# Attention scores in three products a tile: two on all 128 rows, two halves side by side on 64 rows each

## The chip, the cores and the metric

The kernel runs on one core of a Trainium2 chip. The metric is the device time of one execution in microseconds (us), lower being better. Times given are medians of several executions, or, where the profile is quoted, those of the one execution that the hardware profiler recorded.

## The reference

The input is q, k, v of shape (4, 8, 576, 64): four batches, eight heads, 576 tokens, 64 channels. The reference computes, cut to what matters here:

```
scores = matmul(q, k transposed) / 8                 # 576 x 576 for each batch and head
keep the 32 largest scores of each row, softmax over them, attn @ v
x = heads side by side                               # 2304 tokens x 512
x = g(x @ w_in) @ w_out                              # feed-forward, g a clipped square
experts: 8 of them, 288 tokens each, taken in order of the gate's logits; relu(x @ w1[e]) @ w2[e]
```

The choice of the 32 largest and the assignment to experts are discrete, so scores and logits are needed close to float32 precision.

## The kernel before

**Precision by splitting.** TensorE multiplies 32-bit words of the kind `F32R` faster than full float32, but keeps fewer bits of each. The kernel therefore splits a number into an upper part, rounded to what `F32R` keeps, and a lower part, the rest. A product of two split numbers is upper x upper + upper x lower + lower x upper, and the lower x lower term is small.

**Scores.** A pair of heads of one batch is loaded by `load_pair`: for each head the transposed keys (64 channels x 576 tokens) are loaded twice, into rows 0 to 63 and rows 64 to 127 of one raw tile. ScalarE rounds all 128 rows into `k_t`; GpSimd (`G`) then replaces rows 64 to 127 by raw minus rounded. So `k_t` holds upper parts above lower parts. `scores` does the same for a tile of 128 queries: `q_t[:, 0]` holds the upper parts of the queries in both row halves, `q_t[:, 1]` the lower parts in both row halves. A product over all 128 rows of `q_t[:, 0]` with `k_t` gives upper x upper + upper x lower in one go; `q_t[:, 1]` with `k_t` adds lower x upper + lower x lower. The 576 keys are two halves (`hf`) of 288, each in a bank of its own of the accumulator `pS`. A head of a full tile (`j < 4`, 64 such tiles of two heads each, 128 heads in all) thus takes four products of 128 rows x 288 columns: two for each half, each half a group of its own. The fifth tile of a batch and pair (`j == 4`) holds 64 queries of both heads and has its own products of both.

**After the scores.** ScalarE copies both halves of `pS` to `s`, VectorE folds the halves with a maximum (and for some with a minimum) into `f` (the tensors `f<-pS,s` in the profile), searches `f` for the 32 largest, ScalarE and GpSimd make the softmax, `values` transposes it (`pPT`) and multiplies it with v (`pQ`; there the two heads use 64 columns of the array each, and the last 64 tokens 64 rows and 64 columns each). After every 256 tokens comes `ffn_block`, whose products go to `pH` and `pX`. A second part, from some 843 us on, routes tokens to experts and runs the experts.

**Order.** Nothing is issued at once. `_Recorder` notes each instruction with a cost in ns, `Program.add` finds the dependences, and `Program.issue` makes a list schedule from costs, latencies and ranks, improves it over ten rounds, and writes the order of every engine from it. What stands under one `P.group()` stays together. The cost of an `F32R` product of n columns is `10 + 0.43 * n` ns whatever its rows. Because all instructions are recorded by one helper, every one has line 267 in the profile; tensors tell them apart. `pS<-XB` are the score products (keys and queries both lie in `XB`).

Of the kernel before, what the change touches and what calls it, by code (L numbers as in the profile page):

```python
# [15 lines left out]
ALU = mybir.AluOpType  # L16
AX = mybir.AxisListType.X

B, H, S, D = 4, 8, 576, 64
# [193 lines left out]
class _Recorder:  # L213
# [5 lines left out]
    def __getattr__(self, method):  # L219
        def rec(*args, **kw):  # L220
            P, eng = self._prog, self._eng
            reads, writes = [], []
            for i, a in enumerate(args):
                if hasattr(a, "ap"):
                    (reads if i else writes).append(a)
            for k, a in kw.items():
                if hasattr(a, "ap"):
                    (writes if k in self.OUT else reads).append(a)
            if method == "matmul" and not kw["start"]:
                reads.append(writes[0])  # L230
            n = max(_free(a) for a in (writes[:1] if eng == "tensor" else reads + writes))
            inp = any(a.tensor.space == bass.MemoryType.PSUM for a in reads if hasattr(a.tensor, "space"))
            lat = None
            if eng == "vector":
                cost = 69 + 1.04 * n
                if method == "match_replace":
                    cost += 64
                if method == "tensor_scalar" and not inp:
                    cost = 69 + 0.52 * n
                if method == "scalar_tensor_tensor" and not inp:  # L240
                    cost = 69 + (1.04 if kw["in1"].dtype == I32 else 1.2) * n
                if method in ("tensor_tensor", "tensor_copy") and all(
                        x.dtype == BF16 and list(x.ap)[-1][0] == 1 for x in reads + writes):
                    cost = 69 + 0.52 * n
            elif eng == "scalar":
                cost = (51 if inp else 187) + 0.833 * n
                if not inp and args[2] in (AF.Copy, AF.Abs):
                    cost -= 93
                if "accum_out" in kw:
                    cost += 93  # L250
            elif eng == "gpsimd":
                cost = 148 + 2.1 * n
            elif eng == "sync":
                cost = max(60, 128 * min(_free(a) for a in reads + writes) * 4 / 360.0)
                lat = 2000 + 128 * min(_free(a) for a in reads + writes) * 4 / 180.0
            elif method == "transpose":
                cost = 109
            else:
                f32 = args[1].dtype == F32
                if args[1].dtype == F32R:  # L260
                    cost = 10 + 0.43 * n
                else:
                    cost = 2 * max(107, n * 2 / 2.4) + 1 if f32 else max(36, n / 2.4 + 3, 0.5 * _free(args[1]))
                if f32 and args[1].shape[-1] <= 64:
                    cost *= 0.63
            fn = getattr(getattr(P.nc, eng), method)
            P.add(eng, lambda: fn(*args, **kw), cost, reads, writes, lat)  # L267
        return rec


def _free(ap):
    n = 1
    for x in list(ap.shape)[1:]:
        n *= x
    return n
# [3 lines left out]
def kernel(ctx: ExitStack, tc: tile.TileContext, qm, qt, kT, vm, vt,  # L279
# [7 lines left out]
    pS = psum.tile([128, 2, 512], F32, name="pS")  # L287
# [68 lines left out]
    HW = S // 2  # L356
    P = Program(nc, LATX, False)
    V, A, G, T, Y = P.vector, P.scalar, P.gpsimd, P.tensor, P.sync
# [70 lines left out]
    def load_pair(b, p):  # L429
        ks = []  # L430
        for i in range(2):
            raw = t_kr() if b else t_f()
            for z in range(2):
                Y.dma_start(out=raw[64 * z:64 * z + 64, :], in_=kT[b, 2 * p + i])
            k_t = t_k()
            A.activation(k_t, raw, AF.Copy)
            G.tensor_tensor(out=k_t[64:, :], in0=raw[64:, :], in1=k_t[64:, :], op=ALU.subtract)
            ks.append(k_t)
        v_t, u_t = t_v(), t_u()
        if not b:  # L440
            P.rank = max(KR[p], 0.0) - KR[4]
        Y.dma_start(out=v_t, in_=vm[b, :, p])
        Y.dma_start(out=u_t[:, 0, :], in_=vt[b, :, p])
        Y.dma_start(out=u_t[:64, 1, :], in_=vt[b, 64:, p])
        KV[b, p] = (ks, v_t, u_t)

    def scores(b, j, p, r, exact):
        f = []  # L450
        ks = KV[b, p][0]
        full = j < 4
        w = 128 if full else 64
        P.rank = r + R_QL if r else KR[0]
        raw = t_qr()
        for z in range(2):
            Y.dma_start(out=raw[64 * z:64 * z + 64, :, :w], in_=qm[b, j, p] if full else qt[b, p])
        P.rank = r + R_QS
        q_t = t_q()
        qz = [q_t[:, z].rearrange("p i x -> p (i x)").rearrange("p (a x) -> p a x", x=w) for z in range(2)]  # L460
        if not full:
            V.tensor_scalar(q_t.rearrange("p z i x -> p z (i x)")[:, :, 64:192],
                            ones_f.unsqueeze(1).to_broadcast([128, 2, 128]), 0.0, None, op0=ALU.mult)
            qz = [q[:, 0::3, :] for q in qz]
        A.activation(qz[0], raw[:, :, :w], AF.Copy)
        G.tensor_tensor(out=qz[1], in0=raw[:, :, :w], in1=qz[0], op=ALU.subtract)
        s_sb = t_s()
        P.rank = r + R_QK
        for i in range(2 if full else 1):
            for hf in range(2):  # L470
                parts = [(i, 0, hf * 288, 288)]
                if not full:
                    parts += (((1, 0, 64, 288),), ((1, 0, 352, 224), (1, 224, 0, 64)))[hf]
                with P.group():
                    for x, (k, o_, c0, n) in enumerate(parts):
                        for z in range(2):
                            T.matmul(pS[:, hf, o_:o_ + n], q_t[:, z, k, :], ks[k][:, c0:c0 + n],
                                     start=(x + z == 0), stop=(x == len(parts) - 1 and z == 1))
            A.activation(s_sb[:, i, :].rearrange("p (a x) -> p a x", a=2), pS[:, :, :288],
                         AF.Copy if exact else AF.Relu)  # L480
            if not exact:
                f.append(t_f())
                V.tensor_tensor(out=f[i][:, :HW], in0=pS[:, 0, :HW], in1=s_sb[:, i, HW:], op=ALU.max)
                if fold_dve(b, j, p, i):
                    V.tensor_tensor(out=f[i][:, HW:], in0=pS[:, 0, :HW], in1=s_sb[:, i, HW:], op=ALU.min)
        return s_sb, f

    def fold_dve(b, j, p, i):
        return (2 * ((b * 5 + j) * NP + p) + i) % 8 < FOLD_DVE[b]
# [237 lines left out]
    c0, c1 = (t.rearrange("p a x -> p (a x)") for t in s_tiles[:2])  # L727
# [49 lines left out]
    def first_phase(exact):  # L777
        for p in range(NP):
            P.rank = KR[p]
            load_pair(0, p)  # L780
# [7 lines left out]
        for b in range(B):  # L788
            for j in range(5):
                for p in range(NP):  # L790
                    s_sb, f = scores(b, j, p, at, exact)
                    rinv, wide = (topk_exact if exact else topk)(b, j, p, at, s_sb, f)
                    values(b, j, p, at, s_sb, rinv, wide)
                    at += 1.0 if j < 4 else 0.6
                    if j == 4 and b + 1 < B:
                        P.rank = at + R_K
                        load_pair(b + 1, p)
                    if p == NP - 1 and (b, j) == (B - 1, 4):
                        if not exact:
                            find_flag()  # L800
                        k, P.rank = late.pop()
                        ffn_end(k, [pS[:, t] for t in range(2)])
                    if p == NP - 1:
                        while (blk + 1) * BLK <= b * S + min(128 * j + 128, S):
                            ffn_block(blk, at + R_F)
                            blk += 1
# [577 lines left out]
```

## Time and profile before

| | |
|---|---|
| median of 3 executions | 1155.2 us (1153.36 to 1155.45) |
| the profiled execution: its time, its span | 1158.43 us, 1156.7 us |
| TensorE busy (weight loads apart) | 1058.1 us (91%) |
| TensorE weight loads | 939.7 us (81%) |
| VectorE, ScalarE, GpSimd busy | 929.1 (80%), 804.0 (70%), 699.8 us (61%) |
| granted TensorE clock, mean | 0.95 of full speed |

The span runs from the first to the last instruction; the execution's time has 1.7 us around it. A matmul's record runs from its start to a modelled end, and matmuls overlap in the array, so "busy" hides how fast they follow each other: that is read from the distance between starts.

### The profile page before, as it was taken

What the parts mean: (1) busy time and instruction counts of PE and PEld (TensorE: products, weight loads), DVE (VectorE), ACT (ScalarE), POOL (GpSimd) and SP (SyncE); (2) the same over time, 40 slices, a digit from 0 to 9 for tenths busy, and PEclk for the clock granted to TensorE, in tenths of its full rate; (3) what the DMA queues carried; (4) which work ended last, traced back from release to release, by engine and by line L of the source; (5) the groups of instructions that cost most, each with busy time, mean ns of one, the idle gap of its engine ahead of it and who ended that gap; (6) DMA issues with size and microseconds to landing.
All of it is one profiled execution on the core that took longest, in us unless ns stands there. A gap on an engine that the chain in (4) does not pass through costs nothing. (4 is left out here: it accounts for less than half of the span.)

```text
span 1156.7 us, 24352 instructions
## 1 busy us (share of the span) xinstructions
PE 1058.1 (91%) x8331; PEld 939.7 (81%) x8331; DVE 929.1 (80%) x2908; ACT 804.0 (70%) x1835; POOL 699.8 (61%) x872
## 2 busy tenths in 40 slices
PE   2687689999999999999999999999985999999996
PEld 1565588888888888898898888888964899999995
DVE  6889999899989989988989999984346987776530
ACT  6889997888888888867888988964301654445541
POOL 5978898987776987757688778764202122233111
PEclk9956799999999999999999999999987899999998
DMA  9644442352222252222134211211315654555500
GB/s 245 206 133 142 128 133 83 107 159 69 74 66 64 79 175 80 76 81 86 60 100 128 92 56 67 78 61 63 128 41 162 224 173 167 187 188 196 177 23 24
DMA packets 61920, 132.39 MB, mean 114 GB/s; under 512 B 15952, under 2 KB 24400, under 8 KB 61776
## 3 DMA queue, kind: packets, MB, share of 16 engines
q1 hardware_dynamic: 58704, 121.21, 33.4%
q0 software_dynamic: 3072, 9.44, 2.4%
q8 instruction: 69, 1.13, 0.4%
q14 instruction: 75, 0.61, 0.2%
HBM read 116.98 MB, written 13.63 MB: 113 GB/s over the span
## 5 line engine op out<-in xcount | busy, mean ns | idle before, releaser
L267 PE MATMUL pH<-XB,W 128*128 128x256 f32 (+1 forms) x2496 | 361.3, 293 | 3.3 <-DVE XB L267 2.5
L267 PEld LDWEIGHTS pH<-XB,W 128*128 128x128 f32 x2496 | 329.1, 191 | 11.3 <-issue 2.9
L267 DVE MAX8 m<-f 128x8 f32<-128x288 f32 x720 | 300.9, 447 | 2.4 <-POOL f L267 0.4
L267 POOL TENSOR_TENSOR s<-s,f 128x576 f32<-128x576 f32 x144 | 203.7, 1428 | 30.2 <-ACT f L267 29.6
L267 DVE MATCH_REPLACE8 f<-m,f 128x288 f32<-128x288 f32 x432 | 189.9, 442 | 0.1
L267 PE MATMUL pX<-W,XB 128*128 128x512 f32 x608 | 186.3, 411 | 4.0 <-DVEq L823 4.0
L267 PE MATMUL pS<-XB 128*128 128x288 f32 (+2 forms) x672 | 145.5, 326 | 47.2 <-DVE f L267 23.6
L267 PEld LDWEIGHTS pS<-XB 128*128 128x128 f32 x672 | 108.1, 202 | 68.8 <-DVE f L267 31.0
L267 POOL TENSOR_TENSOR XB<-stage,XB 128x512 fp32r<-128x512 f32 (+1 forms) x96 | 127.1, 1325 | 60.4 <-ACT XB L267 40.5
L267 ACT ACTIVATE s<-s,sm 128x576 f32<-128x576 f32 x144 | 111.3, 773 | 21.3 <-POOL s L267 21.0
L267 PEld LDWEIGHTS pX<-W,XB 128*128 128x128 f32 x608 | 107.2, 191 | 21.7 <-issue 6.9
L267 ACT ACTIVATE s<-pS 128x576 f32<-128x576 f32 x144 | 92.5, 643 | 29.6 <-PE pS L267 29.3
L267 ACT ACTIVATE f<-s,t_all 128x576 f32<-128x576 f32 x144 | 107.4, 771 | 2.7
L267 PE MATMUL pX<-XB,W 128*128 128x288 f32 x768 | 109.0, 297 | 0.0
L1187 POOL DMA_INDIRECT xg<-dram_x,idx x24 | 36.9, 1538 | 116.8 <-DVE y L267 37.9
L267 DVE TENSOR_TENSOR f<-pS,s 128x288 f32<-128x288 f32 x198 | 86.0, 447 | 26.4 <-ACT s L267 11.3
L267 DVE TENSOR_TENSOR W<-raw,W 128x1024 fp32r<-128x1024 f32 x64 | 76.6, 1217 | 34.5 <-ACT W L267 34.2
L267 PEld LDWEIGHTS pX<-XB,W 128*128 128x128 f32 x768 | 103.5, 188 | 0.0
L1281 POOL DMA_INDIRECT out_dram<-yo,idx x24 | 27.2, 1135 | 120.4 <-ACT yo L267 117.1
L267 ACT ACTIVATE pt<-pPT 128x512 f32<-128x512 f32 x144 | 84.8, 589 | 20.3 <-PE pPT L267 19.3
L267 PE MATMUL pPT<-ident,s 128*128 128x128 f32 x576 | 93.2, 287 | 2.9 <-ACT pt L267 2.3
L267 ACT ACTIVATE XB<-pH 128x288 fp32r<-128x288 f32 x96 | 38.5, 408 | 77.4 <-PE pH L267 74.5
(191 smaller groups left out, 1949.8 us busy)
## 6 DMA issues: line engine op xcount, KB each, us to landing
wl<-dram_wlo SPq DMA_DIRECT2D x64, 512.0 KB, 3.4
raw<-in_w_dram SPq DMA_DIRECT2D x64, 512.0 KB, 4.8
qr<-in_qm_dram SPq DMA_DIRECT2D x128, 64.0 KB, 2.3
stage<-in_w_in_dram SPq DMA_DIRECT2D x14, 512.0 KB, 4.0
stage<-in_w_out_dram SPq DMA_DIRECT2D x14, 512.0 KB, 3.4
stage<-in_kT_dram SPq DMA_DIRECT2D x48, 144.0 KB, 2.8
v<-in_vm_dram SPq DMA_DIRECT2D x16, 256.0 KB, 3.2
dram_wlo<-wl SPq DMA_DIRECT2D x8, 512.0 KB, 3.0
```

The costliest lines, as they stand in the source:

```text
L267: P.add(eng, lambda: fn(*args, **kw), cost, reads, writes, lat)
L1187: return nc.gpsimd.indirect_dma_start(out=xg[:, g, :], out_offset=None, in_=x2d[:, :], in_offset=bass.IndirectOffsetOnAxis(ap=idx[:, g:g + ...
L1281: st = nc.gpsimd.indirect_dma_start(out=out, out_offset=bass.IndirectOffsetOnAxis(ap=idx[:, g:g + 1], axis=0), in_=yo, in_offset=None)
```

## The change

For a full tile, each head's scores become one group. First the upper parts of the queries meet all 128 rows of the keys, for both halves (two products of 128 rows x 288 columns, as before). Then the lower parts of the queries meet the upper parts of the keys alone, on 64 rows: the first half of the keys on rows 0 to 63, the second half on rows 64 to 127. For that, `load_pair` swaps the two parts of the keys in the second half of the columns: there the lower parts lie in rows 0 to 63 and the upper parts in rows 64 to 127, and the subtraction is issued as two instructions of 64 rows x 288 columns. The lower x lower term is no longer computed for full tiles. The tile of 64 queries keeps its products. In the planner an `F32R` product whose weights have at most 64 rows costs half.

```diff
                 if args[1].dtype == F32R:
                     cost = 10 + 0.43 * n
+                    if args[1].shape[0] <= 64:
+                        cost *= 0.5
...
             A.activation(k_t, raw, AF.Copy)
-            G.tensor_tensor(out=k_t[64:, :], in0=raw[64:, :], in1=k_t[64:, :], op=ALU.subtract)
+            for rows, cols in ((slice(64, 128), slice(0, HW)), (slice(0, 64), slice(HW, S))):
+                G.tensor_tensor(out=k_t[rows, cols], in0=raw[rows, cols], in1=k_t[rows, cols], op=ALU.subtract)
...
         for i in range(2 if full else 1):
-            for hf in range(2):
-                parts = [(i, 0, hf * 288, 288)]
-                if not full:
+            if full:
+                with P.group():
+                    for hf in range(2):
+                        T.matmul(pS[:, hf, :HW], q_t[:, 0, i, :], ks[i][:, HW * hf:HW * hf + HW], start=True, stop=False)
+                    for hf in range(2):
+                        rows = slice(64 * hf, 64 * hf + 64)
+                        T.matmul(pS[:, hf, :HW], q_t[rows, 1, i, :], ks[i][rows, HW * hf:HW * hf + HW],
+                                 start=False, stop=True)
+            else:
+                for hf in range(2):
+                    parts = ((0, 0, hf * HW, HW),)
                     parts += (((1, 0, 64, 288),), ((1, 0, 352, 224), (1, 224, 0, 64)))[hf]
-                with P.group():
...
+                    with P.group():
...
```

## Rows read from the trace of the kernel before

**Rows 1.** Busy time by stretch: PE, PEld, DVE, ACT, POOL, granted clock, DMA, GB/s.
```profile
11.80:200.00 188.20, 142.04 (x875) 116.25 (x876) 173.17 (x520) 168.06 (x423) 161.78 (x189) 0.83 0.49 149
200.00:785.00 585.00, 576.60 (x4599) 502.92 (x4600) 539.07 (x1816) 482.68 (x1138) 451.61 (x587) 0.99 0.28 87
```
**Rows 2.** Waits of PE, then of DVE, from 200 to 785 us: total, times, longest.
```profile
PE pS L267 <- DVE f L267: 6.5, 13, 1.0
...
DVE f L267 <- PE pS L267: 5.5, 10, 1.2
DVE stage L267 <- PE pH L267: 5.1, 9, 1.7
```
**Rows 3.** Waits of PE, then of DVE, from 11.8 to 200 us.
```profile
PE pS L267 <- DVE f L267: 17.1, 12, 3.6
...
DVE f L267 <- PE pS L267: 5.0, 5, 1.9
```
**Rows 4.** The chain that ended last, one stretch of the experts: start, length, products of 288 columns.
```profile
1130.59 12.81 PE pX L267 x96
```
**Rows 5.** Busy time by stretch of the instructions on pS: PE, PEld, DVE, ACT.
```profile
11.80:200.00 188.20, 39.06 (x124) 25.35 (x124) 13.72 (x31) 19.81 (x31) 0.83 0.49 149
```
**Rows 6.** Groups of PE by shape: names, rows*columns of the weights, shape, count, busy, mean ns.
```profile
L267 PE MATMUL pS<-XB 128*128 128x288 f32 x608 | 140.0, 333 | 47.2 <-DVE f L267 23.6 <-ACT XB L267 11.8 <-ACT s L267 10.1
...
L267 PE MATMUL pQ<-tr,u 64*64 64x128 f32 x256 | 29.6, 311 | 0.0
```
**Rows 7.** Timeline of PE, asked in narrow stretches: start, length, count in the stretch.
```profile
407.05 0.29 PE L267 MATMUL pS<-XB 128*128 128x288 f32 x1
...
407.27 0.32 PE L267 MATMUL pQ<-pt,v 128*64 128x128 f32 x1
...
407.86 0.50 PE L267 MATMUL pQ<-pt,v 128*64 128x128 f32 x6
...
408.08 0.28 PE L267 MATMUL pQ<-pt,v 128*64 128x128 f32 x2
...
408.29 0.33 PE L267 MATMUL pQ<-tr,u 64*64 64x128 f32 x2
...
408.45 0.28 PE L267 MATMUL pQ<-tr,u 64*64 64x128 f32 x2
...
408.66 0.33 PE L267 MATMUL pPT<-ident,s 128*128 128x128 f32 x1
```
**Rows 8.** Timeline of PE at 357 us: the same columns.
```profile
357.08 0.53 PE L267 MATMUL pS<-XB 128*128 128x288 f32 x2
357.45 0.76 PE L267 MATMUL pH<-XB,W 128*128 128x256 f32 x5
```
**Rows 9.** Timeline of the weight loads, PEld: start, length, count, idle before and its cause.
```profile
356.71 0.19 PEld L267 LDWEIGHTS pQ<-tr,u 64*64 64x64 f32 x4 [0.17 <-issue]
357.08 0.30 PEld L267 LDWEIGHTS pS<-XB 128*128 128x128 f32 x2 [0.17 <-issue]
...
409.85 0.11 PEld L267 LDWEIGHTS pQ<-ident,s 128*64 128x64 f32 x1
```
**Rows 10.** Waits of PEld from 200 to 785 us.
```profile
PEld pQ L267 <- issue: 16.2, 80, 0.4
```
**Rows 11.** Groups of POOL by shape, 11.8 to 780 us.
```profile
L267 POOL TENSOR_TENSOR f<-f,s 128x288 int32<-128x288 int32 x89 | 71.7, 806 | 1.5
...
L267 POOL TENSOR_TENSOR XB<-stage,XB 64x576 fp32r<-64x576 f32 x24 | 34.2, 1427 | 5.8 <-ACT XB L267 1.7 <-issue 1.7 <-POOL XB L267 1.0
```
**Rows 12.** Timeline of the first score product.
```profile
10.05 1.40 POOL L267 TENSOR_TENSOR XB<-f,XB 64x576 fp32r<-64x576 f32 x1 [9.59 <-ACT XB L267]
...
11.78 0.29 PEld L267 LDWEIGHTS pS<-XB 128*128 128x128 f32 x1 [11.78 <-POOL XB L267]
```

More of the change, by code (lines that the diff above doesn't have):

```diff
@@ L469, in scores @@
         for i in range(2 if full else 1):
-            for hf in range(2):
-                parts = [(i, 0, hf * 288, 288)]
-                if not full:
-                    parts += (((1, 0, 64, 288),), ((1, 0, 352, 224), (1, 224, 0, 64)))[hf]
-                with P.group():
[L475 to L478, printed above, removed]
+            if full:
[9 more added lines that the diff above has]
+                    parts = ((0, 0, hf * HW, HW),)
+                    parts += (((1, 0, 64, 288),), ((1, 0, 352, 224), (1, 224, 0, 64)))[hf]
+                    with P.group():
+                        for x, (k, o_, c0, n) in enumerate(parts):
+                            for z in range(2):
+                                T.matmul(pS[:, hf, o_:o_ + n], q_t[:, z, k, :], ks[k][:, c0:c0 + n],
+                                         start=(x + z == 0), stop=(x == len(parts) - 1 and z == 1))
             A.activation(s_sb[:, i, :].rearrange("p (a x) -> p a x", a=2), pS[:, :, :288],
```

## The prediction

> **What bounds the kernel now.** I read the busy time by stretch first. The page's totals mix several regimes, and the score products don't run in the last of them, so what matters is which engine has no room while they run. From 200 to 785 us the reader is to see that TensorE is busy for 576.6 of 585 us, 8.4 us short of always, at a granted clock of 0.99, while VectorE has 46 us of room and ScalarE and GpSimd over 100 us each [rows 1]. Before 200 us it is the other way round: TensorE lacks 46 of 188 us and VectorE 15, and the clock is 0.83.
>
> A busy share near full can hide slack, because matmul records overlap. So I read the waits next. From 200 to 785 us TensorE's one sizable wait is for VectorE to have read `pS`, 6.5 us in 13 times; VectorE in turn waits 5.5 us for score products and 5.1 us for the feed-forward's [rows 2]. An engine that waits for nobody and that others wait for sets the pace: in this stretch a product added to TensorE lengthens the kernel by nearly its own length, and one removed shortens it until VectorE's 46 us are used up. Before 200 us TensorE waits 17.1 us for VectorE, which waits for it 5.0 us [rows 3], so there TensorE's work is mostly covered.
>
> Last I read starts of single matmuls, because that is where the price of this change lies. What counts is the distance from one start to the next.
>
> **The change part by part.**
>
> *The product removed.* Four products of 288 columns a head become two on 128 rows and two on 64 rows. 96 products of 288 columns in a row take 12.81 us, 0.133 us each [rows 4], so a head costs 4 x 0.133 = 0.533 us now. Up to 200 us there are 124 score products and 31 folds, four products a head, so 31 heads [rows 5]; of 128 heads, 97 come later, where TensorE is the bound.
>
> *The two on 64 rows, side by side.* No product of 64 rows and 128 columns is in this trace. The nearest are those of `values`: 64 columns each, then 64 rows and 64 columns each [rows 6]. They do run side by side: at 408.08 and at 408.29 us two start within a hundredth of a us, and pairs follow at 0.11 us (407.86 to 408.08 us, two pairs) [rows 7], where a single float32 product of 128 columns alone needs that long. So I take the pair of halves at 0.14 us, one product and 0.007 us between the two starts, since the two write different banks. From the other side the bound is 0.267 us, one after the other.
>
> *Going into 64 rows and coming back.* This decides the sum. From the last score product (407.05 us) to the first product with 64 columns (407.27 us) pass 0.22 us, where 0.133 us is due: 0.09 us more. From 64 columns on 128 rows to 64 columns on 64 rows, a change of rows alone, pass 0.21 us (408.08 to 408.29) where 0.11 is due: 0.10 us more. From there back to the whole array again 0.21 us (408.45 to 408.66): 0.10 us more [rows 7]. The weight loads show what is late: those after a change of shape begin only 0.17 us after the previous ones have ended, with no semaphore as the cause [rows 9]; in the stretch there are 80 such waits before `pQ` loads, 16.2 us [rows 10]. So a load is not made ahead across such a change, and it stands open as well: after the way back at 357.08 us, two score products take 0.37 us until the next start (357.45) where 0.267 is due, so 0.10 us of an `F32R` load is exposed [rows 8]; for float32 weights it is 0.05 us (408.29 to 408.45 where 0.11 is due) [rows 7]. I take 0.095 us for a change and 0.10 us for the open load. Below it could be nothing, if 64-row products went through without such a change; the load of 64 columns for a transpose at 409.85 us does pass without any idle time [rows 9], so a smaller operand alone isn't enough to cause it. I stay with the cost, because the pair on rows 64 to 127 has to stand on another part of the array than the whole, as the nearest products do.
>
> The trace prices a change of shape at about 0.1 us [rows 7]. The Trainium skill, TensorEngine Tiling (Array Packing), section Tiling Modes, says that changing the tiling mode, not just the tile, drains the engine; it gives no figure. The trace agrees with it, and by that rule alone the sum would be a loss of unstated size.
>
> So a head after the change: 2 x 0.133, the way in 0.095 + 0.10, the pair 0.14, the way back. The way back costs 0.195 us before an `F32R` product, 0.145 us before a float32 one, and nothing before the products of `values`, which pay for a change now as well; with `F32R` products in the majority I take 0.16 us. The sum is 0.267 + 0.195 + 0.14 + 0.16 = 0.762 us against 0.533: **0.23 us more a head**. For 97 heads that is 22.2 us on the path. Both ends: no change of shape and a full overlap, 0.126 us less a head (12 us less); no overlap and the full price each way, 0.267 + 0.195 + 0.267 + 0.195 = 0.924, 0.39 us more (38 us more).
>
> *One group of four.* Both halves now wait until VectorE has read the first bank. The second half's products could go ahead of that wait before: 13 waits [rows 2] by 0.267 us are 3.5 us at most. Against it, a TensorE that is 22 us later in 585 finds VectorE finished more often, which gives back up to the 6.5 us of those waits. I take 2.5 us back, net.
>
> *The first 200 us.* 31 heads by 0.23 us are 7 us of TensorE work, beside 46 us in which it idles [rows 1]. Only the later end of a head's scores is felt, where VectorE waits for it: 5 waits [rows 3] by 0.23 us are about 1 us; without cover it would be 7 us. I take 1.3 us.
>
> *The keys' subtraction in two.* One of 64 x 576 takes 1.427 us; 288 columns take 0.806 us in the nearest row [rows 11], so 0.19 us more for each of 32 key tiles, 6 us of GpSimd, hidden by the 133 us that it has free from 200 to 785 us [rows 1]. Nothing covers the very first one: the first score product waits at 11.78 us for that subtraction [rows 12], so 0.2 us. If the cover failed throughout it would be 6 us. SP's queue, the transfers and the evictions of `pS` are unchanged in number and size.
>
> *The order.* The planner now counts each product of the pair at half, so it believes that a head saves 0.13 us where I expect it to lose 0.23, and writes a new order for all engines. What an order can shift here is the waits between TensorE and VectorE, 6.5 and 5.5 + 5.1 us [rows 2]; I leave 6 us either way and no middle.
>
> Sum: 22.2 - 2.5 + 1.3 + 0.2 = **21 us more**. The profiled execution took 1158.43 us, its span 1156.7 and 1.7 around it; it becomes 1179.6 us. The median of the runs shown is 3.2 us lower, and on it the forecast is **1176 us**.
>
> **The rivals.**
>
> *No price for the change of shape: faster.* If 64-row products go in and out of the array as those of 128 rows do, a head takes 3 x 0.133 + 0.007. For it speaks the 64-column transpose that passes freely [rows 9]; against it stand all changes of rows or columns that I looked at [rows 7, 9]. 97 x 0.126 = 12 us would leave TensorE; VectorE has 46 us of room there but waits on others besides TensorE, so some of it comes back: 1144 to 1150 us, say 1147. It decides if a change costs less than 0.06 us each way, its open load included. The Trainium skill, TensorE: Matmul & The Clock Gate, section Part 3: Packing small matmuls, states that weights for another row group are loaded while matmuls are in flight and that such tiles start some 4 ns apart; it would make this rival the likely one. The pairs at 0.01 us [rows 7] agree with the second half of it; the 0.17 us before the loads of the 64-row products [rows 9] do not agree with the first.
>
> *The pair one after the other.* Rows are shared out, but all 128 output columns are used by both, which nothing in this trace does. The head then takes 0.127 us more, 12 us over the sum: 1188 us.
>
> *Nothing to be seen.* No price for the change of shape, but no overlap either: four products of 0.133 us as now, and only the 0.2 us at the start, 1155 us. Or the price is paid where TensorE would have waited anyway; for that its 8.4 us of idle time are too few [rows 1].
>
> **How the numbers follow.** The forecast has 0.72; by its own terms it lies between 1166 us (all 6.5 us of waits given back, a favourable order) and 1186 us (the full price each way, an order that costs 6 us). The pair in sequence has 0.08, the free change of shape 0.12, nothing to be seen 0.08, which I split: 0.05 within 0.2% (about what a measurement of this kernel can tell from no change, 2.3 us) and 0.03 a small loss. Slower is 0.72 + 0.08 + 0.03 = 0.83, same 0.05, faster 0.12. The range from 1157 to 1192 us leaves out the faster cases and most of the unchanged, and a tenth of the slowest.
>
> **What the profile would show.** If right: in the stretch of the scores each head has two starts 0.133 us apart, 0.2 us or more to a pair that starts within 0.01 us, then 0.2 us or more to the next product, whose successor is late by an open load; weight loads on `pS` idle with "issue" as the cause, about 0.17 us twice a head; TensorE stays without room after 200 us and the feed-forward after 785 us keeps its length but starts some 20 us later. The step on overlap is wrong if the pair's starts lie 0.12 us apart or more. The step on the change of shape is wrong if loads for the pair begin while the products before still run; then the kernel is faster. The forecast is also wrong if VectorE's busy share rises from 200 to 785 us, since then TensorE was not the bound.

## The result, and the profile after

The changed kernel takes 1169.9 us (median of 6 executions, 1165.84 to 1173.87) against 1154.53 us for the kernel before on the same chip: a ratio of 1.0129 with a 95% interval of 1.0102 to 1.0156, some 15 us slower. The forecast was 1176 us. The profiled execution took 1170.42 us with a span of 1168.6 us; it stands 12.0 us above the profiled one of before, less than the 15.4 us between the medians, because the profiled execution of before was 3.9 us above its own median.

Busy time by stretch in the changed kernel (PE, PEld, DVE, ACT, POOL, clock, DMA, GB/s), the answer to [rows 1]:

```profile
11.80:200.00 188.20, 151.73 (x884) 117.99 (x885) 175.28 (x524) 169.08 (x428) 164.22 (x198) 0.85 0.48 150
200.00:785.00 585.00, 578.92 (x4484) 484.50 (x4483) 527.67 (x1782) 474.40 (x1114) 443.79 (x598) 0.99 0.28 86
```

TensorE is full from 200 to 785 us as before, but starts 4484 matmuls there in place of 4599; VectorE is busy for 11.4 us less in that stretch. TensorE's instructions are as many as before, so the work is later: the last score product starts at 790.5 us, where it was 777.7 us. First the changed kernel's row, then that of before (durations min/median/max, then first and last start):

```profile
L269 PE MATMUL pS<-XB x672: 199/379/610, 12.4 to 790.5; 128*128 128x288 f32 x152, 128*128 128x64 f32 x8, 128*128 128x224 f32 x8
```
```profile
L267 PE MATMUL pS<-XB x672: 199/295/611, 11.8 to 777.7; 128*128 128x288 f32 x152, 128*128 128x64 f32 x8, 128*128 128x224 f32 x8
```

All of the 12 us between the two spans lie up to the last score product, which starts 12.8 us later; what follows it took 379.0 us and takes 378.1. One head of the changed kernel, asked in narrow stretches (start, length, count), answers to [rows 7, 8]:

```profile
306.20 0.29 PE L269 MATMUL pS<-XB 128*128 128x288 f32 x1
...
306.33 0.62 PE L269 MATMUL pS<-XB 128*128 128x288 f32 x3
...
306.56 0.40 PE L269 MATMUL pS<-XB 64*128 64x288 f32 x2
...
306.89 0.50 PE L269 MATMUL pX<-W,XB 128*128 128x512 f32 x1
...
307.23 0.64 PE L269 MATMUL pX<-W,XB 128*128 128x512 f32 x2
```

The two products on 128 rows start 0.13 us apart (306.20, 306.33). To the pair pass 0.23 us, a product and 0.10. Both of the pair start within a hundredth: the view that ends at 306.57 us already counts three products from 306.33 on. To the next product pass 0.33 us, forecast as 0.10 + 0.14 + 0.095, and that product's successor comes after 0.34 us where 512 columns are due in 0.23: the open load, that is a weight load that nothing hides. This head is no exception: over the 97 heads after 200 us the medians are 0.224 us into the pair, 0.003 us within it and 0.329 us to the next product. The weight loads around it (start, length, count, idle before and its cause), then the group of the pairs' loads over the whole run, then the waits from 200 to 785 us, answer to [rows 9, 10]:

```profile
306.56 0.19 PEld L269 LDWEIGHTS pS<-XB 64*128 64x128 f32 x2 [0.16 <-issue]
306.88 0.54 PEld L269 LDWEIGHTS pX<-W,XB 128*128 128x128 f32 x3
```
```profile
L269 PEld LDWEIGHTS pS<-XB 64*128 64x128 f32 x256 | 25.8, 198 | 23.1 <-issue 21.8 <-POOL XB L269 0.6 <-POOL f L269 0.3
```
```profile
PEld pS L269 <- issue: 16.6, 101, 0.3
PEld pQ L269 <- issue: 13.6, 65, 0.4
```

Before the loads of the pairs stand 21.8 us of idle time with no semaphore behind it, 0.17 us for each of 128 trips (a trip is the way into the 64-row products and back). From 200 to 785 us `pS` has 16.6 us of such waits in 101 times, where it had 3.0 us in 13 times; the kernel before had them on `pQ`. What went the other way are TensorE's waits for VectorE and VectorE's for scores. From 200 to 785 us, the longest of PE, and those of DVE that answer to [rows 2]:

```profile
PE pPT L269 <- ACT s L269: 3.5, 3, 1.9
...
DVE f L269 <- PE pS L269: 1.7, 1, 1.7
```

TensorE's 6.5 us of waiting for VectorE to have read `pS` are gone. Its idle time falls by less, from 8.4 to 6.1 us, since waits for ScalarE took part of that place. VectorE's waits for scores have fallen from 5.5 to 1.7 us, but all its waits for TensorE together rose from 18.1 to 26.4 us, those for `pQ` alone by 8 us: VectorE waits for TensorE more than before, not less.

### The profile page after: what moved, and what is told of

Read it like the earlier page. It is cut to its first block, busy times and chain, and to the rows that moved or that the text cites. A ratio compares the mean times of both kernels' runs of the same rounds, so it can differ in the third digit from the quotient of the medians.

```text
span 1168.6 us, 24389 instructions
## 1 busy us (share of the span) xinstructions
PE 1081.8 (93%) x8331; PEld 933.1 (80%) x8331; DVE 929.5 (80%) x2908; ACT 805.8 (69%) x1835; POOL 702.7 (60%) x904
## 5 line engine op out<-in xcount | busy, mean ns | idle before, releaser
L269 PE MATMUL pH<-XB,W 128*128 128x256 f32 (+1 forms) x2496 | 366.9, 296 | 2.5 <-DVE XB L269 2.5
L269 POOL TENSOR_TENSOR XB<-stage,XB 128x512 fp32r<-128x512 f32 (+1 forms) x120 | 131.1, 1093 | 78.2 <-ACT XB L269 36.8
L269 PE MATMUL pS<-XB 128*128 128x288 f32 (+3 forms) x672 | 136.6, 363 | 29.0 <-DVE f L269 14.9
L269 PEld LDWEIGHTS pS<-XB 128*128 128x128 f32 (+1 forms) x672 | 93.2, 201 | 64.1 <-issue 23.9
L269 DVE TENSOR_TENSOR f<-pS,s 128x288 f32<-128x288 f32 x198 | 86.4, 449 | 26.4 <-ACT s L269 13.1
L269 PE MATMUL pQ<-pt,v 128*64 128x128 f32 (+1 forms) x1280 | 91.5, 283 | 2.6 <-ACT tr L269 2.0
```

## The experiments

Ratios are to the kernel before on the same chip, with 95% intervals; microseconds are medians.

### The keys alone

```diff
-            G.tensor_tensor(out=k_t[64:, :], in0=raw[64:, :], in1=k_t[64:, :], op=ALU.subtract)
+            for rows, cols in ((slice(64, 128), slice(0, HW)), (slice(0, 64), slice(HW, S))):
+                G.tensor_tensor(out=k_t[rows, cols], in0=raw[rows, cols], in1=k_t[rows, cols], op=ALU.subtract)
```

> The kernel before with only the keys' second half swapped (subtraction in two instructions of 288 columns); products as before. If the trips to 64 rows are the cause: within 3 us of before (0.2 us at the start, the rest a new order). If the two subtractions or the layout on GpSimd are the cause: some 15 us slower, as the changed kernel.

Measured: 1159.4 us, 1.0034 (1.0023 to 1.0045). The keys are not the 15 us, but they cost 3 to 4 us, a little more than the 3 us that I allowed.

### The two subtractions in the old order

```diff
-            G.tensor_tensor(out=k_t[64:, :], ...)
+            def low(raw=raw, k_t=k_t):
+                for cols in (slice(0, HW), slice(HW, S)):
+                    nc.gpsimd.tensor_tensor(out=k_t[64:, cols], in0=raw[64:, cols], in1=k_t[64:, cols], op=ALU.subtract)
+            P.add("gpsimd", low, 148 + 2.1 * S, [raw[64:, :], k_t[64:, :]], [k_t[64:, :]])
```

> The kernel before, its order of every engine kept word for word, but with the keys' subtraction issued as two instructions of 288 columns on rows 64 to 127. The run with the keys alone came out 3.3 us slower than before, more than its 0.2 us at the start explains. If the two instructions cost that on GpSimd: 3 us slower here too. If it was the newly written order, or the added wait of the next key load for GpSimd: within 1 us of before.

Measured: 1156.82 us, 1.0005 (0.9994 to 1.0016). Two instructions in place of one cost nothing that can be told. In the changed kernel each takes 0.80 us, as taken from [rows 11]:

```profile
L269 POOL TENSOR_TENSOR XB<-stage,XB 64x288 fp32r<-64x288 f32 x48 | 38.5, 802 | 5.5 <-POOL XB L269 1.9 <-POOL sm L269 0.8 <-POOL d_all L269 0.5
```

What the keys alone cost is thus the newly written order or the next key load's wait for GpSimd, which now reads both row halves; the two weren't told apart.

### Three products, no trips

```diff
-                        for z in range(2):
+                        zs = 1 if full and hf else 2
+                        for z in range(zs):
                             T.matmul(pS[:, hf, o_:o_ + n], q_t[:, z, k, :], ks[k][:, c0:c0 + n],
-                                     start=(x + z == 0), stop=(x == len(parts) - 1 and z == 1))
+                                     start=(x + z == 0), stop=(x == len(parts) - 1 and z == zs - 1))
```

> The kernel before with the lower-part product of the second half left out for full tiles (three products of 128 rows a head; the scores of the second half lack that term). It is what the change would give if 64-row products went in and out freely. If TensorE is the bound after 200 us: 97 x 0.133 = 13 us leave it, and the time falls by 6 to 13 us (1142 to 1149); the changed kernel is then 21 to 28 us above it, the price of 97 trips. If TensorE is not the bound: within 3 us of before, and the changed kernel's loss has to come from elsewhere.

This kernel leaves out a term of half of the scores and serves for its time alone. Measured: 1143.04 us, 0.9893 (0.9869 to 0.9918): 12.4 us faster, where 13 us of products leave TensorE after 200 us. In the profiled executions 10.9 us are gained from the 31st head to the last score product (567.9 us in place of 578.8), and 6 us before, where 31 products less are 4 us (a new order is in both). So TensorE is the bound after 200 us, its work is not quite free before, and the change's own saving is real; without the price of the trips about the time of the rival "faster" would have come out (it said 1144 to 1150 us).

### The planner's cost undone

```diff
-                    if args[1].shape[0] <= 64:
-                        cost *= 0.5
```

> The changed kernel with the planner's halved cost taken out, so that a 64-row product counts as one of 128 rows. If the trips are the cause: still 10 to 18 us slower than before. If the order written from costs that are too low is the cause: within 4 us of before.

Measured: 1173.84 us, 1.0154 (1.014 to 1.0168). An order written from the full cost is no better, so the halved cost isn't what makes the loss. A planner that knows the price of a trip, and could for instance put the pairs of two heads into one trip, was not tried.

### Two trips a head

```diff
                     for hf in range(2):
                         T.matmul(pS[:, hf, :HW], q_t[:, 0, i, :], ...)
-                    for hf in range(2):
                         rows = slice(64 * hf, 64 * hf + 64)
                         T.matmul(pS[:, hf, :HW], q_t[rows, 1, i, :], ...)
```

> The changed kernel with the group in another order: first half on 128 rows, its 64-row product, second half on 128 rows, its 64-row product. No two 64-row products side by side, two trips a head in place of one. If a trip costs 0.36 us: a head takes 4 x 0.133 + 2 x 0.195 in + 0.195 and 0.16 out = 1.28 us, 0.52 more than in the changed kernel, 50 us on 97 heads: about 1215 to 1225 us. If the changes of shape are free and only the overlap matters: 0.13 us a head, 12 us, about 1182 us.

Measured: 1236.91 us, 1.0682 (1.0655 to 1.0709), 64 us (by the ratios) to 67 us (by the medians) over the changed kernel. Every engine works off the same order as in the changed kernel, so a new order has no part in this. One head, asked as above:

```profile
332.21 0.29 PE L269 MATMUL pS<-XB 128*128 128x288 f32 x1
...
332.44 0.72 PE L269 MATMUL pS<-XB 64*128 64x288 f32 x2
332.76 0.72 PE L269 MATMUL pS<-XB 128*128 128x288 f32 x2
...
333.09 0.39 PE L269 MATMUL pS<-XB 64*128 64x288 f32 x1
333.41 0.50 PE L269 MATMUL pX<-W,XB 128*128 128x512 f32 x1
```

In: 0.23 us (332.21 to 332.44). Then 0.32 and 0.33 us and, to 333.41, again 0.32: each of the three changes behind it costs a product, 0.09 and an open load. From the first product to the one behind the head pass 1.20 us (332.21 to 333.41), in the changed kernel 0.69 (306.20 to 306.89): 0.51 us more, forecast as 0.52. The total was not the forecast one, because I counted 97 heads: 128 heads at 0.51 us are 65 us. At this price the first 200 us no longer cover the trips: TensorE starts 778 matmuls there, 875 before [rows 1], and the last product of the 31st head ends at 215.5 us, where it ends at 197.4 in the changed kernel, 18 us later for 31 x 0.51 = 16 us.

```profile
11.80:200.00 188.20, 159.65 (x778) 117.63 (x778) 163.76 (x478) 158.95 (x400) 149.73 (x180) 0.96 0.47 143
```

### The pair on the same rows

```diff
-                        rows = slice(64 * hf, 64 * hf + 64)
+                        rows = slice(0, 64)
```
(and the keys' subtraction as before)

> The changed kernel with both 64-row products on rows 0 to 63, the keys laid out as before: the same trip, no overlap. If the overlap is worth one product: 0.13 us a head more than in the changed kernel, 12.5 us on 97 heads, about 1182 us, and the starts of the two 0.13 us apart. If the two halves weren't really overlapping, or TensorE has slack: the changed kernel's time within 4 us.

Measured: 1186.27 us, 1.0259 (1.0245 to 1.0274), 0.0130 over the changed kernel, 15 us, where 12.5 were expected; a new order is in this difference. The overlap of the two halves is real and worth about one product a head. One head:

```profile
301.47 0.53 PE L269 MATMUL pS<-XB 64*128 64x288 f32 x2
...
301.71 0.29 PE L269 MATMUL pS<-XB 64*128 64x288 f32 x1
301.93 0.50 PE L269 MATMUL pX<-W,XB 128*128 128x512 f32 x1
```

The second of the two (301.71) starts 0.24 us after the first (301.47): the product's 0.133 and the open load, which then is not open a second time, since to the way back pass 0.22 us, a product and 0.09.

### The group of four alone

```diff
-                        rows = slice(64 * hf, 64 * hf + 64)
-                        T.matmul(pS[:, hf, :HW], q_t[rows, 1, i, :], ks[i][rows, HW * hf:HW * hf + HW],
-                                 start=False, stop=True)
+                        T.matmul(pS[:, hf, :HW], q_t[:, 1, i, :], ks[i][:, HW * hf:HW * hf + HW], start=False, stop=True)
```
(against the changed kernel; the keys' subtraction as before)

> The changed kernel's group of four and its order of products, but all four on 128 rows and the keys laid out as before: the group alone. If the trips are the cause, and the group's wait for VectorE costs at most 3.5 us: between 3 us under and 5 us over before (a new order is written too). If the group of four behind VectorE is what makes the changed kernel slow: some 15 us over before.

Measured: 1148.03 us, 0.9922 (0.9905 to 0.9939): 8 to 9 us *faster* than before. For the group itself I had allowed a cost alone, up to 3.5 us; the 2.5 us that I took back net were to come from a TensorE that is late. It isn't late here, and the group gains. The waits of PE from 200 to 785 us, and of DVE for scores, answer to [rows 2]:

```profile
PE pS L269 <- DVE f L269: 2.9, 7, 0.6
...
DVE f L269 <- PE pS L269: 0.8, 1, 0.8
```

What the group ends is seen in the kernel before at 413 us (PE and ACT):

```profile
413.06 0.53 PE L267 MATMUL pS<-XB 128*128 128x288 f32 x2
...
414.29 0.51 PE L267 MATMUL pS<-XB 128*128 128x288 f32 x2
...
415.53 0.64 ACT L267 ACTIVATE s<-pS 128x576 f32<-128x576 f32 x1
```

and in the group of four at 412 us:

```profile
412.05 0.76 PE L269 MATMUL pS<-XB 128*128 128x288 f32 x4
```

Before, a head's first half was done early, held its bank and served nobody, because ScalarE reads both halves at once: from the start times, 55 of the 97 heads after 200 us had other products between their first and last, and the four starts spread over 1.26 us on average. In the group of four it is 0 of 96 and 0.43 us. Of the gain 3 to 5 us are there by the 31st head (its copy ends 2.9 us earlier than before, its last product 5.0), the rest comes from there to the last score product. Before 200 us VectorE gets 4.4 us more done (177.55 us against 173.17 in [rows 1]), and its 5.0 us of waits for scores there [rows 3] are gone. After it, TensorE waits for VectorE 2.9 us against 6.5, but its idle time falls only from 8.4 to 6.8 us.

```profile
11.80:200.00 188.20, 147.29 (x909) 122.91 (x909) 177.55 (x526) 169.28 (x427) 163.06 (x192) 0.83 0.49 151
200.00:785.00 585.00, 578.20 (x4653) 504.70 (x4650) 541.62 (x1830) 486.70 (x1151) 453.94 (x590) 1.00 0.28 89
```

Another part of the gain is in the distances of starts, which the waits don't count. Where score products come behind other work, mostly behind float32 products or a change of shape, the second of them often starts 0.21 to 0.24 us after the first in place of 0.133 (two products in 0.37 us at 357.08 in [rows 8] are such a case). A head whose halves are apart pays this up to twice: from 200 to 785 us there are 79 such late starts before and 45 in the group of four, 3.6 us less in sum.

### The group with its sequence changed

Both against the group of four; in the first, the order written for every engine is the same as there.

```diff
-                    for hf in range(2):
-                        T.matmul(..., q_t[:, 0, i, :], ...)
-                    for hf in range(2):
-                        T.matmul(..., q_t[:, 1, i, :], ...)
+                    for hf in range(2):              # the second run: for hf in (1, 0)
+                        for z in range(2):
+                            T.matmul(pS[:, hf, :HW], q_t[:, z, i, :], ..., start=not z, stop=z == 1)
```

> The group of four on 128 rows again, its products in the sequence of before: first half upper and lower, then second half upper and lower. The order of all engines is the same as in the group of four. If keeping a head's four products together is what made that run 8 us faster: the same time within 2 us, about 1148 us. If the sequence of the products mattered (two with the same weights in a row): back to 1153 to 1157 us.

> The group of four on 128 rows with the second half of the keys ahead of the first. The bank of the second half is free once ScalarE has read it, the first half's only after VectorE. If the group's wait for VectorE still costs something: up to 3 us faster than the group of four, the 2.9 us that TensorE waits there after 200 us. If not: the same within 2 us.

Measured: 1148.26 us, 0.994 (0.9928 to 0.9952), and 1146.9 us, 0.9932 (0.9919 to 0.9945). The sequence inside the group hardly matters; it is the keeping together. The second run was to take the group's wait for VectorE away, and did not. TensorE's longest wait from 200 to 770 us is the same line in both:

```profile
PE pS L269 <- DVE f L269: 3.0, 7, 0.6
```

So what that wait costs is not shown.

### Luck of the order

```diff
-                    cost = 10 + 0.43 * n
+                    cost = 12 + 0.43 * n
```

> The kernel before with one planner constant moved, an F32R product counted at 12 + 0.43 n ns in place of 10 + 0.43 n: the same instructions in another order, a measure of what any newly written order changes. If orders differ by a few us at random: 1151 to 1161 us, with about half of the heads' products apart as before. If the group's gain was only the luck of a new order, gains of 8 us should be as easy to get here: 1148 us or so.

> The group of four on 128 rows with the same constant moved. If the group gives the gain: 5 us or more under the other order of before, 1146 to 1152 us. If it was the luck of one order: about the time of before, 1154 to 1160 us.

Measured: before in another order 1158.49 us, 1.0029 (1.0018 to 1.0041), with 52 of 97 heads apart; the group in another order 1146.56 us, 0.9924 (0.9908 to 0.9941). A new order moved the kernel before by 3 us the wrong way, and the group's gain was there under both orders, 8 and 12 us. As far as two orders of each can tell, the order's luck is a few us, and the group is not luck.

### The changed kernel with its groups apart

```diff
-                with P.group():
-                    for hf in range(2):
+                for hf in range(2):
+                    with P.group():
                         T.matmul(pS[:, hf, :HW], q_t[:, 0, i, :], ...)
+                with P.group():
                     for hf in range(2):
                         ...
```

> The changed kernel with three groups a head in place of one: each half's 128-row product alone, the 64-row pair together, so that the second half need not wait for VectorE to read the first bank. If the group's wait costs something now: up to 3.5 us faster than the changed kernel. If TensorE, being later, finds VectorE done anyway: within 4 us of it either way (new order).

Measured: 1175.04 us, 1.0152 (1.0133 to 1.0172), against 1.0129 (1.0102 to 1.0156) for the changed kernel: not faster, and whether slower can't be told from the ratios. With the trips in the kernel, then, the group is worth some 3 us, not clear of noise, and less than the 8 to 9 us without them. 62 of 97 heads are apart again, and VectorE waits 14.0 us for scores from 200 to 785 us where the changed kernel shows 1.7:

```profile
DVE f L269 <- PE pS L269: 14.0, 19, 1.5
```

## Why the prediction was right, point by point

**TensorE is the bound after 200 us: right.** Taking a product a head away gave 12.4 us where 13 were on the path, and in the changed kernel VectorE's busy time in the stretch fell, as the forecast asked.

**The trip's price: right, in each of its parts.** The way in, the overlapped pair, the way out and the open load were read from other products of the kernel before, and the changed kernel shows them within 0.01 us, in the medians over 97 heads. The run with two trips, in the same order as the changed kernel, adds 0.51 us a head where 0.52 were worked out. Against the group of four on 128 rows, which differs by the trips, the keys' layout and a newly written order, the changed kernel stands at 1.0129 to 0.9922, or 1169.9 to 1148.0 us: 22 to 24 us, where 97 x 0.23 = 22.2 us were worked out. The keys alone, with an order of their own, cost 3 to 4 us; what part of that is in the 22 to 24 was not told apart. A change of rows alone does have a price, so the rival without one fell, and the pair does overlap, so the rival in sequence fell; the price of going in and out takes nearly three of such savings (0.36 us against 0.126, both as worked out). One reading in that rival was wrong: the 0.17 us before the loads of 64-row products [rows 9] were held against loading weights for one half of the rows beside work on the other. But the products ahead of those loads stand on all 128 rows, so this row says nothing on that case. Within the pair, the changed kernel makes its two loads in 0.19 us together (306.56), about the time of one.

**The group of four: mis-sized.** "I take 2.5 us back, net", between a cost of 3.5 and a gain of 6.5 us. The net sign was right, the parts were not: for the group itself I saw a cost alone, and measured alone it gives back 8 to 9 us (0.9922), 12 under the other order. I asked only what the second half would lose by waiting for the first half's bank, and not what the first half gains by not going ahead; the wait of ScalarE for the whole of `pS` should have told me that half a head serves nobody. The later TensorE gave back 2.3 us of idle time, not up to 6.5. Whether this term is why the time came out at 1169.9 and not at 1176 us is not shown: beside the trips, taken from the changed kernel with its groups apart, the group is worth some 3 us, close to the 2.5, and then it is the rest that was taken too dear: that kernel is 18 to 19 us over before, where trips and keys were put at 23.7. The runs do not show that the two effects add up.

**The first 200 us: right in the main.** VectorE got 175.28 us done there against 173.17 before, but the group of four without trips got 177.55. The changed kernel is behind that one by 1.4 us (the 31st head's copy) to 3.5 us (its last product), where 1.3 us were forecast and 7 would be due without cover. The run with two trips a head shows where the cover ends.

**The keys' subtraction: right for the two instructions, not for the layout.** 0.80 us each, hidden; the two in the old order cost 0.05% (-0.06 to 0.16). Swapped as in the change, and with a new order, the keys cost 3 to 4 us where 0.2 were forecast; the cause stays open.

**The order: right in the size left for it:** 3 us between two orders of the kernel before, and 4 us between the changed kernel's two, within the 6 allowed. It is not the cause of the 15 us.

In sum: +22 to 24 us for the trips (with the keys' layout and an order), 8 to 9 us back from the group, 15 us measured. That these add up is no test, since both were taken against the same run, the group of four. The sum by its own terms was 21: the direction and the mechanism were right, and that a total 6 us too high stayed so near owes something to terms that were off in both directions.

## What to carry to other kernels

A product on part of the array saves time only if enough of them share one trip: here a trip cost 0.36 us and each overlapped pair saved 0.126, so by these numbers fewer than three pairs a trip lose (no run here had more than one). The price could be read beforehand from the other products on part of the array, by the distance of starts on either side of them. When an edit also changes what stays together in the schedule, time that alone: the best version here is the kernel before with a head's four products on 128 rows kept in one group, 1147 to 1148 us, 0.6 to 0.8% under before. And cover has an edge: before 200 us one trip a head showed with 1.4 to 3.5 us of its 7, and the 16 us more of two trips in full.

## What the runs showed that I had not expected

Two products on the same 64 rows do not start one product apart after a way in, but 0.24 us: the first one's record begins with its open load, so a start-to-start distance across a change of shape holds the load and not the product alone. And half a head computed early was worth less than nothing, at least without the trips, under both orders. From 200 to 785 us VectorE waited 5.4 to 14.0 us for scores in the runs with the products of a head apart, at most 2.8 us in those with them together; that these waits are what the group saves is not shown, for TensorE is the bound there, and part of the gain is in its own late starts.
